# A planner that counts a shared port, with new durations, and integer additions that may run on VectorE

## The chip, the core and the metric

The kernel runs on one core of one Trainium2 chip. The core has five engines, each with its own queue of instructions that it takes in order: TensorE (PE in the rows, with its weight loads as PEld), VectorE (DVE), ScalarE (ACT), GpSimdE (POOL) and SyncE (SP, whose queue issues the DMAs). The metric is the device time of one execution in microseconds (us), the median of several runs.

## What is computed

Inputs are float32 for attention and 8-byte floats for the weights. For each of 4 batches and 8 heads, attention over 576 positions of width 64 keeps only scores within tau of the row's maximum; the 2304 tokens of width 512 that result go through two dense blocks:

```
scores = scale * np.matmul(q, k.transpose(0, 1, 3, 2))
thresh = np.max(scores, axis=-1, keepdims=True) - tau
scores = np.where(scores >= thresh, scores, -1e9)
x = softmax(scores) @ v                      # (2304, 512)
h = x @ w_in                                 # (2304, 2048)
x = (np.maximum(h, 0) + alpha * np.minimum(h, 0)) @ w_out
a, b = x @ w1, x @ w2                        # (2304, 1024) each
out = ((a * b) @ w3) @ w_out2                # (2304, 512)
```

## The kernel before

**Stages.** Attention comes first; its order of instructions is fixed by a table of numbers. The dense part follows on the same core, and the change is about that part. TensorE's first dense matmul starts 317 us after the first instruction.

**Tokens.** They are cut into five tiles: four of 512 (one for a batch) and one of 256 (the last 64 positions of each batch). The first dense stage takes them in the order 0, small tile, 1, 2, 3; the second in the order 0 to 3, small tile.

**Matmuls.** Each float32 operand is split into a high and a low part (hi and lo), and three products of parts stand for one product: 12 matmuls for a group of 128 rows of weights, 512 tokens and four blocks of 128. For each of 16 blocks f of the hidden width the first stage does a group "h" (x times w_in), then side (L925, ACT) and the leaky step (L930, DVE), both of which read PSUM, then hi and lo of the result g (helpers split_hi, L175 to L181, and split_lo, L184), and a group "acc" (times w_out). The second stage folds w3 and w_out2 into one matrix first, then does for 8 blocks a group for a, one for b, their product (L1047, L1050), its split, and a group of the output. The four or five rows named h, acc, gs, x, wa, wu and wp in the trace are these: h and acc are PSUM banks, x, gs the split activations, wa, wu, wp the split weights.

**Weights.** They arrive as 8-byte floats and are converted to float32 by integer operations: cvt_low (L192, ACT) brings the lower word to its place, cvt_high makes four steps on the upper word (L198 on ACT or L200 on DVE, then L203, L205, L209 on DVE), and cvt_round adds the two as integers (L214, on POOL always). The loads go into two buffers named raw, the result is a tile m of which there are three. Fourteen of the 16 blocks of w_in are converted during attention; the last two and the 16 of w_out while the first tile runs; w1, w2, w_out2 and w3, 40 tiles in all, behind that: these are converted once, stored to DRAM (L801) and loaded again later (z, L815). The 16 tiles of w3 are turned by TensorE before they are stored (four 128x128 transposes of a tile, L787).

**What sets the order.** A planner inside the kernel, list_order, makes the order of the dense part when the program is built. Each piece of work is an Op with the engines that can do it and a duration for each, a priority, the Ops it depends on, and the buffer it takes. The planner takes, again and again, the Op that can start first by its own clock (a little dearer where it has a choice of engines), puts it on the engine that starts it first, and so decides both the engine and the place in each engine's queue. On the chip every engine then follows its queue in that order and waits for what each instruction needs. The durations stand in the calls of op(...) in weight, halves, put_by, split and in the loops; MM is the time of one matmul of 512 columns. In the planner before, every engine is free when its own last Op has ended.

## Time and profile before

| what | value |
|---|---|
| median of 3 runs | 1092.97 us (1091.52 to 1093.36) |
| profiled execution, its own time | 1092.37 us |
| its span, first to last instruction | 1090.6 us |
| PE busy | 1047.3 us, 96% |
| DVE busy | 698.4 us, 64% |
| ACT busy | 440.0 us, 40% |
| POOL busy | 389.6 us, 36% |
| mean granted TensorE clock | 0.99 of full speed |

The shares are averages over stages with different limits: in attention all engines are busy, in the second dense stage hardly any but TensorE. What a stage loses is read from TensorE's rows in order of time: the start of one group of matmuls to the start of a later one, against the number of groups between. A matmul's own row overlaps the next one's by a little, so starts are compared, not durations. "Granted clock" is the share of full speed that the chip gave TensorE.

### The profile page before, as it was taken

What the parts mean: (1) busy time and instruction counts of PE and PEld (TensorE: products, weight loads), DVE (VectorE), ACT (ScalarE), POOL (GpSimd) and SP (SyncE); (2) the same over time, 40 slices, a digit from 0 to 9 for tenths busy, and PEclk for the clock granted to TensorE, in tenths of its full rate; (3) what the DMA queues carried; (4) which work ended last, traced back from release to release, by engine and by line L of the source; (5) the groups of instructions that cost most, each with busy time, mean ns of one, the idle gap of its engine ahead of it and who ended that gap; (6) DMA issues with size and microseconds to landing.
All of it is one profiled execution on the core that took longest, in us unless ns stands there. A gap on an engine that the chain in (4) does not pass through costs nothing.

```text
span 1090.6 us, 16110 instructions
## 1 busy us (share of the span) xinstructions
PE 1047.3 (96%) x5792; PEld 857.1 (79%) x5792; DVE 698.4 (64%) x1479; ACT 440.0 (40%) x840; POOL 389.6 (36%) x445
## 2 busy tenths in 40 slices
PE   4999999999989989999999999999999999999997
PEld 4877777777768769888867788888888888888896
DVE  5999999999869999987677545754322322223122
ACT  3989889898854443333233212211100201111020
POOL 3777787777543444544343112301200101000000
PEclk9999999999999998999989999999999999999999
DMA  3535252524213335545334202323100100001010
GB/s 93 148 85 145 78 153 77 149 81 130 51 59 109 104 116 170 178 156 181 107 137 145 78 1 58 97 68 97 39 1 1 39 1 10 29 1 39 1 39 20
DMA packets 62383, 89.14 MB, mean 82 GB/s; under 512 B 13920, under 2 KB 42592, under 8 KB 62304
## 3 DMA queue, kind: packets, MB, share of 16 engines
q1 hardware_dynamic: 60096, 88.10, 26.7%
q8 instruction: 46, 0.75, 0.3%
q10 hardware_dynamic: 2208, 0.01, 0.1%
q14 instruction: 33, 0.27, 0.1%
HBM read 62.40 MB, written 15.20 MB: 71 GB/s over the span
## 4 chain that ended last, share of the span: by engine, by line
PE 52%; DVE 4%; DMA 2%; POOL 1%; issue 1%; ACT 1%; SPq 0%; POOLq 0%; DVEq 0%; ACTq 0%
PE h L858 32%; PE acc L858 19%; DMA raw<-in_moe_w_dram 2%; POOL m L214 1%; DVE m L209 1%; DVE g L930 1%; DVE m L203 1%; DVE m L205 1%; DVE x L184 0%; PE h L787 0%; ACT raw L192 0%; DVE m L200 0%; ACT g L925 0%; DVE gs L181 0%; DVE gs L184 0%
## 5 line engine op out<-in xcount | busy, mean ns | idle before, releaser
L858 PE MATMUL h<-x,wa 128*128 128x512 f32 (+1 forms) x1920 | 418.4, 371 | 2.7 <-DVE x L184 1.3
L858 PEld LDWEIGHTS h<-x,wa 128*128 128x128 f32 x1920 | 337.4, 190 | 65.6 <-POOL x L184 2.2
L858 PE MATMUL acc<-gs,wu 128*128 128x512 f32 (+1 forms) x960 | 215.9, 373 | 9.4 <-POOL gs L184 4.8
L858 PEld LDWEIGHTS acc<-gs,wu 128*128 128x128 f32 x960 | 169.0, 190 | 44.8 <-POOL gs L184 8.3
L1050 DVE TENSOR_TENSOR ab<-h,ab 128x512 f32<-128x512 f32 (+1 forms) x40 | 25.5, 638 | 206.2 <-PE h L858 200.1
L184 POOL TENSOR_TENSOR x<-xT,x 128x512 fp32r<-128x512 f32 (+1 forms) x18 | 21.6, 1205 | 299.0 <-ACT x L179 251.7
L214 POOL TENSOR_TENSOR m<-m,raw 128x512 int32<-128x512 int32 x58 | 79.4, 1368 | 119.1 <-DVE m L209 86.8
L401 ACT ACTIVATE e<-s_ps,sm 128x576 f32<-128x576 f32 x144 | 107.1, 752 | 30.8 <-DVE sm L390 30.1
L438 POOL TENSOR_SCALAR p<-p,sm 128x576 f32<-128x576 f32 x128 | 94.1, 748 | 70.1 <-DVE sm L431 61.2
L390 DVE TENSOR_REDUCE sm<-s_ps 128x1 f32<-128x576 f32 x144 | 106.3, 747 | 19.2 <-PE s_ps L368 19.1
L1047 ACT COPY ab<-h 128x512 f32<-128x512 f32 (+1 forms) x38 | 20.6, 542 | 223.0 <-PE h L858 219.0
L858 PE MATMUL acc<-wp,gs 128*128 128x512 f32 x432 | 104.8, 390 | 0.9 <-DVE gs L181 0.9
L415 DVE SCALAR_TENSOR_TENSOR p<-s_ps,sm,e 128x576 f32<-128x576 f32 x128 | 101.9, 806 | 0.9 <-ACT e L401 0.6
L925 ACT ACTIVATE g<-h,sign_sb 128x512 f32<-128x512 f32 (+1 forms) x80 | 51.3, 641 | 120.4 <-PE h L858 102.2
L455 PE MATMUL pt_ps<-ident,p 128*128 128x128 f32 x576 | 89.6, 280 | 8.4 <-ACT pt L469 7.2
L858 PEld LDWEIGHTS acc<-wp,gs 128*128 128x128 f32 x432 | 80.5, 188 | 17.4 <-DVE gs L181 1.1
L482 PE MATMUL pv_ps<-pt,vraw 128*64 128x256 f32 (+1 forms) x640 | 84.5, 411 | 0.0
L368 PE MATMUL s_ps<-kT,qT 128*128 128x288 f32 x320 | 80.2, 333 | 3.5 <-DVE sm L393 1.7
L455 PEld LDWEIGHTS pt_ps<-ident,p 128*128 128x128 f32 x576 | 64.9, 141 | 21.0 <-ACT pt L469 11.8
L930 DVE SCALAR_TENSOR_TENSOR g<-h,salpha_sb,g 128x512 f32<-128x512 f32 (+1 forms) x80 | 55.5, 693 | 37.3 <-ACT g L925 37.2
L192 ACT ACTIVATE raw<-raw 128x512 int32<-128x512 uint32 x58 | 39.2, 679 | 81.8 <-DMA raw<-in_moe_w_dram 37.5
L368 PE MATMUL s_ps<-kT,qU 128*128 128x288 f32 x320 | 69.7, 300 | 2.3 <-DMA qU<-qT 2.3
(101 smaller groups left out, 1267.4 us busy)
## 6 DMA issues: line engine op xcount, KB each, us to landing
raw<-in_moe_w_dram SPq DMA_DIRECT2D x32, 512.0 KB, 3.8
raw<-in_moe_w_out_dram SPq DMA_DIRECT2D x24, 512.0 KB, 3.5
qU<-qT SPq DMA_DIRECT2D x32, 320.0 KB, 3.9
z<-w SPq DMA_DIRECT2D x40, 256.0 KB, 2.7
wraw<-in_moe_w_in_dram SPq DMA_DIRECT2D x14, 512.0 KB, 4.1
w<-m SPq DMA_DIRECT2D x24, 256.0 KB, 2.2
qraw<-in_q_dram SPq DMA_DIRECT2D x16, 256.0 KB, 4.1
kraw<-in_k_dram SPq DMA_DIRECT2D x16, 256.0 KB, 4.4
```

Of the source, the lines that this page charges most:

```text
L192: nc.scalar.activation(out=c, in_=low, func=AF.Copy, scale=2.0**-29)
L214: nc.gpsimd.tensor_tensor(out=mc[0], in0=mc[0], in1=mc[1], op=ALU.add)
L368: nc.tensor.matmul(out=sp[:, j, 0:HS], lhsT=d[t][:, hh, c * 128 : (c + 1) * 128], rhs=d["kT"][:, hh, k0 + j * HS : k0 + (j + 1) * HS], sta ...
L390: nc.vector.tensor_reduce(out=sm_of(u, 0), in_=st[u], axis=AX.XY, op=ALU.max, negate=True)
L401: nc.scalar.activation(out=es[u].rearrange("p (j s) -> p j s", j=2), in_=st[u], func=AF.Exp, bias=sm_of(u, 0))
L415: nc.vector.scalar_tensor_tensor(out=p_at(u).rearrange("p (j s) -> p j s", j=2), in0=st.pop(u), scalar=sm_of(u, 1), in1=es.pop(u).rearrang ...
L438: nc.gpsimd.tensor_scalar(out=out, in0=in_, scalar1=sm_of(u, 3), scalar2=1.0, op0=ALU.mult, op1=ALU.mult)
L455: nc.tensor.transpose(t[:, i, :], p[:, at + i * 128 : at + (i + 1) * 128], ident)
L482: nc.tensor.matmul(out=o[64 * hh : 64 * hh + 64, 0:n], lhsT=vr[:, hh, i, :], rhs=pt[:, 0 if i == 4 and not half else hh, i, :], start=(i = ...
L858: nc.tensor.matmul(out=out, lhsT=l, rhs=r, start=first and i == 0, stop=last and i == n - 1)
L925: nc.scalar.activation(out=gt()[:, 0:n], in_=ps()[:, 0:n], func=AF.Copy, scale=sign_sb[:, f : f + 1])
L930: nc.vector.scalar_tensor_tensor(out=gt()[:, 0:n], in0=ps()[:, 0:n], scalar=salpha_sb[:, f : f + 1], in1=gt()[:, 0:n], op0=ALU.mult, op1=A ...
```

## The change

Four things change in the planner and the calls, and nothing in what is computed.

1. Each Op has a mark, port, which is set for work that reads and writes SBUF alone and cleared where PSUM is read (copies from PSUM, the leaky step, the product of a and b, the split of the folded matrix). A marked Op on VectorE starts, by the planner's clock, only when the last marked Op on GpSimdE has ended, and the other way round.
2. The durations: a matmul 0.227 instead of 0.2163, work of 128x512 on GpSimdE 1.27 instead of 1.22, and on VectorE and ScalarE up to 0.07 more than before.
3. cvt_round takes an engine. In the dense part the planner may put the integer addition on GpSimdE (1.27) or VectorE (0.61). During attention it stays on GpSimdE.
4. Line numbers move by 6 above the planner's use (L184 becomes L190, L209 L215, L214 L220) and by 12 below (L858 becomes L870, L930 L942).

```diff
@@ list_order
+    shared = {"V": 0.0, "P": 0.0}
...
                 start = max([at, free_at.get(e, 0.0)] + ...)
+                if o.port and e in shared:
+                    start = max(start, shared["P" if e == "V" else "V"])
...
         free_at[e] = o.end
+        if o.port and e in shared:
+            shared[e] = o.end
@@ cvt_round
-    def cvt_round(mc):
-        nc.gpsimd.tensor_tensor(out=mc[0], in0=mc[0], in1=mc[1], op=ALU.add)
+    def cvt_round(eng, mc):
+        eng.tensor_tensor(out=mc[0], in0=mc[0], in1=mc[1], op=ALU.add)
         return mc[0].bitcast(F32)
@@ the dense part
-        MM = 0.2163
+        MM = 0.227
-        def op(engines, emit, prio, deps=(), take=None, free=()):
+        def op(engines, emit, prio, deps=(), take=None, free=(), port=True):
@@ weight
-            c = op({"A": 0.52}, low, prio, [ld])
+            c = op({"A": 0.57}, low, prio, [ld])
-            m = first = op({"V": 0.34, "A": 0.52}, lambda e: high(e, 0), prio, [ld], take="m")
+            m = first = op({"V": 0.34, "A": 0.55}, lambda e: high(e, 0), prio, [ld], take="m")
-                m = op({"V": 0.6 if i == 3 else 0.31}, ...)
-            a = op({"P": 1.22}, add, prio + 1, [c, m], free=[ld])
+                m = op({"V": 0.61 if i == 3 else 0.343}, ...)
+            a = op({"P": 1.27, "V": 0.61}, add, prio + 1, [c, m], free=[ld])
@@ halves
-            h = op({"A": 0.6} if signed else {"A": 0.52, "V": 0.335}, hi, ...)
-            l = op({"V": 0.6} if signed else {"P": 1.22, "V": 0.6}, lo, ...)
+            h = op({"A": 0.63} if signed else {"A": 0.52, "V": 0.336}, hi, ...)
+            l = op({"V": 0.665} if signed else {"P": 1.27, "V": 0.61}, lo, ...)
@@ split
-            lo_on = {"V": part(n, 0.66 if psum else 0.6)}
+            lo_on = {"V": part(n, 0.66 if psum else 0.61)}
             if not psum:
-                lo_on["P"] = part(n, 1.22)
+                lo_on["P"] = part(n, 1.27)
@@ first dense stage
-                u = op({"A": part(n, 0.57)}, side, now + 2.8, [hj], take="u")
-                g = op({"V": part(n, 0.61)}, prelu, now + 3.5, [u], free=[hj])
+                u = op({"A": part(n, 0.585)}, side, now + 2.8, [hj], take="u")
+                g = op({"V": part(n, 0.66)}, prelu, now + 3.5, [u], free=[hj], port=False)
```

How the order moves, at two places. In the names, m is a conversion's tile, raw its load, wu and wa split weights, gs and x split activations, g the leaky step's result, h a PSUM bank.

The first place is in the first token tile, where TensorE works on the blocks f while w_out is converted for later ones. VectorE's queue before, from one block to the next (two conversions, one split of gs):

```order
L203 TENSOR_SCALAR m_4869<-m_4869 128x512
L205 TENSOR_SCALAR m_4869<-m_4869 128x512
L209 SCALAR_TENSOR_TENSOR m_4869<-raw_4828,m_4869 128x512
L181 CAST gs_4890<-g_4865 128x512
L184 TENSOR_TENSOR gs_4890<-g_4865,gs_4890 128x512
L203 TENSOR_SCALAR m_4888<-m_4888 128x512
L205 TENSOR_SCALAR m_4888<-m_4888 128x512
L209 SCALAR_TENSOR_TENSOR m_4888<-raw_4850,m_4888 128x512
L758 SCALAR_TENSOR_TENSOR wu_4896<-m_4869,sign_sb_61,wu_4896 128x512
L930 SCALAR_TENSOR_TENSOR g_4913<-h_4873,salpha_sb_62,g_4913 128x512
```

GpSimdE's queue before, in the same stretch, with the additions of both conversions (m_4869, m_4888) and a subtraction of gs:

```order
L214 TENSOR_TENSOR m_4869<-m_4869,raw_4828 128x512
L214 TENSOR_TENSOR m_4888<-m_4888,raw_4850 128x512
L184 TENSOR_TENSOR gs_4935<-g_4913,gs_4935 128x512
L214 TENSOR_TENSOR m_4940<-m_4940,raw_4910 128x512
L214 TENSOR_TENSOR m_4962<-m_4962,raw_4920 128x512
```

VectorE's queue in the change, for the same two blocks of w_out (there m_4869 and m_4890):

```order
L215 SCALAR_TENSOR_TENSOR m_4869<-raw_4840,m_4869 128x512
L206 TENSOR_SCALAR m_4890<-raw_4862 128x512
L209 TENSOR_SCALAR m_4890<-m_4890 128x512
L211 TENSOR_SCALAR m_4890<-m_4890 128x512
L215 SCALAR_TENSOR_TENSOR m_4890<-raw_4862,m_4890 128x512
L942 SCALAR_TENSOR_TENSOR g_4906<-h_4871,salpha_sb_62,g_4906 128x512
L220 ISA m_4869<-raw_4840,m_4869 128x1024
L220 ISA m_4890<-raw_4862,m_4890 128x1024
L187 CAST gs_4930<-g_4906 128x512
L764 SCALAR_TENSOR_TENSOR wu_4926<-m_4869,sign_sb_61,wu_4926 128x512
L764 SCALAR_TENSOR_TENSOR wu_4932<-m_4890,sign_sb_61,wu_4932 128x512
L190 TENSOR_TENSOR gs_4930<-g_4906,gs_4930 128x512
```

GpSimdE's queue in the change, where the dense part begins:

```order
L220 TENSOR_TENSOR m_4647<-m_4647,raw_4617 128x512
L220 TENSOR_TENSOR m_4799<-m_4799,raw_4770 128x512
L190 TENSOR_TENSOR gs_4885<-g_4860,gs_4885 128x512
L220 TENSOR_TENSOR m_5026<-m_5026,raw_5000 128x512
L220 TENSOR_TENSOR m_5095<-m_5095,raw_5067 128x512
```

The additions of this pair have moved from GpSimdE to VectorE (the two ISA rows, which write the 512 words of m as 1024 half-words), and GpSimdE's queue, which held every conversion's addition in turn, goes from m_4647 to m_4799 and then to m_5026.

The second place is where tile 2 of the first dense stage begins. x is split anew, while w3 is converted and TensorE stands ready for a transpose. VectorE's queue before:

```order
L209 SCALAR_TENSOR_TENSOR m_6696<-raw_6649,m_6696 128x512
L181 CAST x_6734<-xT2_73 128x512
L181 CAST x_6736<-xT2_73 128x512
L930 SCALAR_TENSOR_TENSOR g_6732<-h_6706,salpha_sb_62,g_6732 128x512
L181 CAST x_6746<-xT2_73 128x512
L181 CAST gs_6750<-g_6732 128x512
L184 TENSOR_TENSOR x_6742<-xT2_73,x_6742 128x512
L203 TENSOR_SCALAR m_6748<-m_6748 128x512
L205 TENSOR_SCALAR m_6748<-m_6748 128x512
L209 SCALAR_TENSOR_TENSOR m_6748<-raw_6694,m_6748 128x512
L184 TENSOR_TENSOR gs_6750<-g_6732,gs_6750 128x512
```

GpSimdE's queue before, there:

```order
L214 TENSOR_TENSOR m_6696<-m_6696,raw_6649 128x512
L184 TENSOR_TENSOR x_6734<-xT2_73,x_6734 128x512
L184 TENSOR_TENSOR x_6736<-xT2_73,x_6736 128x512
L184 TENSOR_TENSOR x_6746<-xT2_73,x_6746 128x512
L214 TENSOR_TENSOR m_6748<-m_6748,raw_6694 128x512
L184 TENSOR_TENSOR gs_6804<-g_6781,gs_6804 128x512
```

VectorE's queue in the change (x_6731 to x_6739 are the same four parts of x):

```order
L215 SCALAR_TENSOR_TENSOR m_6722<-raw_6665,m_6722 128x512
L187 CAST x_6733<-xT2_73 128x512
L942 SCALAR_TENSOR_TENSOR g_6728<-h_6703,salpha_sb_62,g_6728 128x512
L220 ISA m_6722<-raw_6665,m_6722 128x1024
L190 TENSOR_TENSOR x_6731<-xT2_73,x_6731 128x512
L190 TENSOR_TENSOR x_6733<-xT2_73,x_6733 128x512
L190 TENSOR_TENSOR x_6737<-xT2_73,x_6737 128x512
L190 TENSOR_TENSOR x_6739<-xT2_73,x_6739 128x512
L190 TENSOR_TENSOR gs_6741<-g_6728,gs_6741 128x512
```

Three of the four subtractions of x have moved from GpSimdE to VectorE, behind the tile's last leaky step and the addition of the conversion that the next transpose reads; GpSimdE has no instruction at this place. In TensorE's queue of the change a group acc and a transpose stand between the last group h of the tile and the first of the next, and the acc that reads the last gs follows that.

## Rows read from the trace of the kernel before

**Rows 1.** Busy time by stage: engines' us (instructions), granted clock, DMA share, GB/s.
```profile
core 0: us, PE busy (x) PEld busy (x) DVE busy (x) ACT busy (x) POOL busy (x), PEclk, DMA share, GB/s
317.00:414.00 97.00, 90.13 (x376) 71.25 (x375) 90.86 (x128) 43.20 (x71) 42.67 (x31) 0.97 0.33 105
414.00:465.00 51.00, 48.39 (x384) 47.10 (x384) 46.95 (x86) 19.76 (x40) 22.86 (x19) 1.00 0.54 173
...
555.00:612.00 57.00, 52.46 (x230) 40.79 (x229) 41.12 (x63) 19.32 (x32) 21.98 (x17) 0.94 0.37 128
612.00:1086.00 474.00, 472.54 (x2174) 394.57 (x2172) 170.58 (x284) 67.63 (x114) 42.37 (x30) 1.00 0.10 32
```

**Rows 2.** TensorE in order of time, first and last dense matmuls: start, us, what.
```profile
317.12 0.97 PE L858 MATMUL h<-x,wa 128*128 128x512 f32 x3
...
1083.81 1.65 PE L858 MATMUL acc<-wp,gs 128*128 128x512 f32 x6 [0.92 <-DVE gs L181]
```

**Rows 3.** Chain that ended last, in order of time: start, us, what.
```profile
574.76 0.44 PE h L787 x4
...
620.39 2.72 PE h L858 x12
...
1067.30 1.43 PE h L858 x12
```

**Rows 4.** TensorE in order of time, end of the first tile.
```profile
362.45 2.88 PE L858 MATMUL h<-x,wa 128*128 128x512 f32 x12
...
407.33 0.56 PE L858 MATMUL acc<-gs,wu 128*128 128x512 f32 x1 [2.42 <-ACT gs L179]
408.87 5.06 PE L858 MATMUL acc<-gs,wu 128*128 128x512 f32 x11 [0.97 <-POOL gs L184]
413.73 0.63 PE L858 MATMUL h<-x,wa 128*128 128x256 f32 x2
```

**Rows 5.** TensorE in order of time, end of the small tile.
```profile
454.23 1.60 PE L858 MATMUL h<-x,wa 128*128 128x256 f32 x12
...
465.07 1.09 PE L858 MATMUL h<-x,wa 128*128 128x512 f32 x4
```

**Rows 6.** TensorE in order of time, w3's transposes (L787) among the groups.
```profile
553.72 1.39 PE L858 MATMUL h<-x,wa 128*128 128x512 f32 x4
...
557.71 2.43 PE L858 MATMUL h<-x,wa 128*128 128x512 f32 x5 [1.34 <-DVE x L184]
560.98 1.12 PE L787 MATMUL h<-ident,m 128*128 128x128 f32 x4 [0.84 <-POOL m L214]
...
611.95 5.72 PE L858 MATMUL h<-x,wa 128*128 128x512 f32 x24
```

**Rows 7.** All engines in order of time, 370 to 373.5 us.
```profile
370.54 1.42 POOL L214 TENSOR_TENSOR m<-m,raw 128x512 int32<-128x512 int32 x1 [0.63 <-DVE m L209]
370.83 1.42 DVE L203 TENSOR_SCALAR m<-m 128x512 f32<-128x512 f32 x1
...
372.28 0.43 DVE L205 TENSOR_SCALAR m<-m 128x512 int32<-128x512 int32 x1
372.74 0.69 DVE L209 SCALAR_TENSOR_TENSOR m<-raw,m 128x512 int32<-128x512 int32 x1
```

**Rows 8.** All engines in order of time, 353.9 to 356.5 us.
```profile
354.00 0.74 DVE L758 SCALAR_TENSOR_TENSOR wu<-m,sign_sb,wu 128x512 fp32r<-128x512 f32 x1
...
354.31 1.60 POOL L214 TENSOR_TENSOR m<-m,raw 128x512 int32<-128x512 int32 x1 [2.31 <-DVE m L209]
354.66 0.74 DVE L930 SCALAR_TENSOR_TENSOR g<-h,salpha_sb,g 128x512 f32<-128x512 f32 x1
```

**Rows 9.** VectorE by line and form, 620 to 1091 us: count, busy us, mean ns, idle before.
```profile
L184 DVE TENSOR_TENSOR gs<-g,gs 128x512 fp32r<-128x512 f32 x22 | 15.2, 690 | 0.5
...
L181 DVE CAST gs<-g 128x512 fp32r<-128x512 f32 x23 | 9.8, 426 | 22.6 <-PE acc L858 22.5
```

**Rows 10.** GpSimdE by line and form, 335 to 1091 us.
```profile
L214 POOL TENSOR_TENSOR m<-m,raw 128x512 int32<-128x512 int32 x55 | 75.1, 1366 | 112.4 <-DVE m L209 86.8 <-issue 8.3 <-ACT raw L192 7.6
```

**Rows 11.** GpSimdE in order of time, the step to tile 2.
```profile
552.69 2.66 POOL L184 TENSOR_TENSOR x<-xT,x 128x512 fp32r<-128x512 f32 x2 [0.36 <-DVE x L181]
...
559.32 1.61 POOL L214 TENSOR_TENSOR m<-m,raw 128x512 int32<-128x512 int32 x1 [2.21 <-DVE m L209]
```

More of the change, by code (lines that the diff above doesn't have):

```diff
@@ L25, with __init__ @@
 class Op:
-    def __init__(self, engines, emit, prio, deps=(), take=None, free=()):
-        self.engines, self.emit, self.prio, self.take = engines, emit, prio, take
+    def __init__(self, engines, emit, prio, deps=(), take=None, free=(), port=False):
+        self.engines, self.emit, self.prio, self.take, self.port = engines, emit, prio, take, port
         self.deps, self.free = list(dict.fromkeys(deps)), list(free)
@@ L703 @@
         NT = len(tiles)
-        MM = 0.2163
+        MM = 0.227
         ops = []
-        def op(engines, emit, prio, deps=(), take=None, free=()):
-            ops.append(Op(engines, emit, prio, deps, take, free))
+        def op(engines, emit, prio, deps=(), take=None, free=(), port=True):
+            ops.append(Op(engines, emit, prio, deps, take, free, port))
             return ops[-1]
@@ L794, in put_by @@
                 t = op({"T": 0.44}, tr, prio + 2, [a], take="h", free=[first])
-                a = first = op({"A": 0.48, "V": 0.6}, ev, prio + 3, [t], take="m", free=[t])
+                a = first = op({"A": 0.48, "V": 0.6}, ev, prio + 3, [t], take="m", free=[t], port=False)
             else:
@@ L974 @@
                 x_ready[t].append(
-                    op({"A": part(n, 0.48), "V": part(n, 0.6)}, ev, now + 1.5 * dt, [xj], free=[acc_op])
+                    op(
+                        {"A": part(n, 0.48), "V": part(n, 0.6)},
+                        ev,
+                        now + 1.5 * dt,
+                        [xj],
+                        free=[acc_op],
+                        port=False,
+                    )
                 )
@@ L1091, in store @@
                             nc.sync.dma_start(out=out[r0 : r0 + ST, :], in_=o()[64 * j : 64 * j + 64])
-                v = op({"A": 0.48, "V": 0.6}, ev, now + dt / 2 + 0.1 * m, [oj], take="u", free=[acc_op])
+                v = op({"A": 0.48, "V": 0.6}, ev, now + dt / 2 + 0.1 * m, [oj], take="u", free=[acc_op], port=False)
                 st_ = op({"S": 0.65 if t < B else 1.3}, store, now + dt / 2 + 0.5, [v])
```

22 lines of the change are left out of this document (14 added, 8 removed).

## The prediction, made before the changed kernel was run

> **What bounds the kernel now.** I read the busy table by stage first, then TensorE's row of instructions in order of time, then VectorE and GpSimdE beside each other. The reader is to see that TensorE sets the end: in the dense part it works from 317.12 us to 1083.81 + 1.65 = 1085.46 us [rows 2], 768.3 us. The work there is fixed. The first stage has 16 blocks x 4 tiles x 24 matmuls of 512 columns and 16 x 24 of 256; the second has 192 and 4 x 8 x 36 of 512, and 8 x 24 of 256 with 8 x 6 of 512 for the small tile; together 2928 of 512 columns, 576 of 256, and 16 transposes of a 512-column block. Twelve of 512 columns take 2.72 us, twelve of 256 1.43 to 1.44 (I take 1.44), a block's transposes 0.44 [rows 3]: 244 x 2.72 + 48 x 1.44 + 16 x 0.44 = 739.8 us. So 28.5 us of the dense part are lost, and they lie in few places:
>
> - End of the first token tile: from 362.45 to 413.73 [rows 4] there are 15 groups of twelve, 40.8 us in 51.3: **10.5 us lost**. The waits named are for ACT gs and POOL gs, the split of the activations, and eleven matmuls then take 5.06 us instead of 2.5: the granted clock is down (0.97 over the stage [rows 1], at half speed for a while after the long wait).
> - Small tile to next tile: 454.23 to 465.07 [rows 5], 5 groups of 1.44 in 10.84 us: **3.6 us lost**.
> - Conversions of w3, with TensorE's transposes among the matmuls: 553.72 to 611.95 [rows 6], 16 groups and 10 transposes, 43.5 + 4.4 in 58.2 us: **10.3 us lost**, with a wait for DVE x, one for POOL m (the conversion's addition), and half clock again (0.94 in this stage [rows 1]).
>
> That makes 24.4 us; the other 4.1 us lie at the first matmuls, the last group and in small pieces, and from 612 us on TensorE is busy 472.5 of 474 us [rows 1].
>
> Why the partners are late is in the two engines' rows. A POOL addition starts at 370.54 and takes 1.42; the DVE instruction that starts at 370.83 takes 1.42 and ends when POOL does, where the same kind takes 0.43 just after [rows 7]. A DVE instruction that reads PSUM (L930) takes 0.74 in the middle of a POOL addition [rows 8]: it is not held. So SBUF-to-SBUF work of the two engines goes one after the other, and POOL's price is 1.37 for an addition [rows 10] where DVE has 0.69 for a subtraction of the same size [rows 9].
>
> **The change, part by part.** Attention's order is untouched; only the dense part's order moves. The order shows 44 of its 58 integer additions on DVE, and 48 fewer subtractions on POOL (of 128x512 and 128x256). I set demand against supply, in each place as (DVE time) + (POOL time) with nothing beside nothing, and again without the L930 rows, which POOL can run beside.
>
> *First tile, from its first to its 16th L930:* supply is 15 steps x 5.44 = 81.6 us. Prices: L200, L203, L205 0.43, L209 0.69 [rows 7], L758 0.74, L930 0.74 [rows 8], the cast (hi) 0.43, the subtraction (lo) 0.69 [rows 9], POOL 1.37 [rows 10].
> Before: 50 x 0.43 + 18 x 0.69 + 16 x 0.74 + 15 x 0.74 + 10 hi x 0.43 + 9 lo x 0.69 = 67.3 on DVE, 26 x 1.37 = 35.6 on POOL: 91.8 without L930, 102.9 with it, over the supply by 10.2 to 21.3. The 10.5 us lost sit at the lower end, which says that L930 really hides.
> After: 47 x 0.43 + 16 x 0.69 + 15 x 0.74 + 15 x 0.74 + 7 x 0.43 + 16 lo x 0.69 + 13 additions = 67.5 + 13 x 0.69 = 76.5 on DVE, 5 x 1.37 = 6.9 on POOL: 72.3 without L930, 83.4 with it: between 9.3 us to spare and 1.8 too much. At the end where before sits, nothing is lost; I leave 1.0 us for bunches (the order puts eight conversion instructions between two L930). **Gain 9.5.**
>
> *The addition's own price* is the one unknown: no row has an integer addition on DVE, and the order shows it as an instruction of another form that writes 1024 half-words. It reads and writes the same bytes as L209 (every second word of raw, and m, 512 results), 0.69; as twice as many elements it would be 2 x 0.69 = 1.38. I take 0.69, since L209 is the nearest row, and keep 1.38 as a rival. The strided operand costs nothing by the rows: L209 at 0.69 is no slower than the contiguous subtraction at 0.69. The Trainium skill (Vector Engine (DVE) Microarchitecture Reference, section 5.2, Measured stream behaviour on trn2) says otherwise: a port keeps its full rate only on pairs of adjacent words, and one source that hops at every element gives 1.73 ns a column, an estimate of 512 x 1.73 + 75 ns = 0.96 us; by it the first tile's additions would cost 3.5 us more, inside what is to spare, and w3's transposes some 2 us, about 1076 in all. The trace disagrees with it on L209, and the trace decides.
>
> *Small tile to next tile:* the change runs three of the four subtractions of x and most of gs on DVE, and TensorE has five groups of 1.44 to cover them instead of four. Three lo and one hi on DVE are 2.5 us and one lo on POOL 1.37, together 3.9 under 7.2 us, beside gs of the small tile. I leave 1.5 of 3.6 us. **Gain 2.1.**
>
> *w3's stretch:* at the step to the third large tile POOL did three subtractions of x, two of them for 2.66 us from 552.69 [rows 11], and the addition that the transpose waits for came behind them. In the changed order the addition and all four lo follow on DVE: behind the tile's last h come ACT 0.7, L930 0.74, addition 0.69, four lo 2.8, gs lo 0.69 = 5.6 us, and TensorE has a group, a transpose and a group to do meanwhile, 2.72 + 0.44 + 2.72 = 5.9. It fits by 0.3 us, so small waits stay; ten or more transposes stand singly between groups and each can wait a little. No wait comes near the 2.4 and 1.3 us [rows 4, 6] behind which the clock fell. I leave 3.0 of 10.3 us. **Gain 7.3.**
>
> *At nothing:* the eight subtractions of wu moved to DVE lie after 612 us, where DVE is busy 171 of 474 us [rows 1]; if that cover failed it would cost 8 x 0.69 = 5.5 us. The new durations and the new time of a matmul in the planner act through the order alone. Casts moved to ACT (ten of gs in the first tile instead of nine, two of wa) cost ACT little; it is busy 43 of 97 us there [rows 1].
>
> Sum: 9.5 + 2.1 + 7.3 = 18.9. The profiled execution took 1092.37 us, 0.6 below the median of the runs, 1092.97; 1092.4 - 18.9 = **1073.5 us**. If all 24.4 went, and with them a little of the rest, 1067.
>
> **Rivals.**
>
> 1. *The addition costs 1.38.* For it: 1024 elements written; against: the bytes are L209's. The first tile's demand rises by 13 x 0.69 = 9.0 us, from 9.3 to spare to 0.3 at the lower end; I put 3 us of loss. Each transpose of w3 waits directly for an addition: 16 x 0.69 = 11 us at most, half of it 5.5, with 3 us as in the forecast and a half-clock stretch of 3.4 (0.06 of 57 us [rows 1]). With 2.5 at the small tile, 17 of 24.4 us stay: about 1085. The Trainium skill (VectorE: DVE Perf Modes, Mode 2x_1P) gives 16-bit operands with step 1 two results a cycle, which would make 1024 half-words as quick as 512 words and the sum the forecast's; no row here shows that mode.
>
> 2. *The clock falls once more at w3.* The fit of 0.3 us fails: a raw load lands late, or the two raw buffers hold a conversion up, and one wait of over 2 us brings a half-clock stretch. For it: in this stretch the changed order gives TensorE's transposes no slack. Price 3 + 3.4: about 1080.
>
> 3. *Slower: VectorE becomes the bound.* The mechanism is the same addition at a far higher price, in place of POOL's 1.37. Room is 9.3 us in the first tile (13 additions) and, by the same sum without L930, 3 in the small tile (5 additions, 46 us of supply for 43) and 12 in the second large one (17 additions, 91 for 79 us). The 24.4 us are eaten when 35 (p - 0.69) = 24.4 + 24.3, at p = 2.1 us; at 2.5 it would be 35 x 1.81 - 48.7 = 14.7 us slower, about 1107. For it: a form no row shows. Against: nothing of 512 words on DVE takes over 0.75 unheld.
>
> 4. *No change:* the lost time is the conversions' loads, not the port. Against: the waits name POOL and DVE results, and the held instructions end with POOL's. About 1092.
>
> **How the numbers follow.** Forecast (1067 to 1078) 0.62; clock falls 0.14; addition at 1.38 0.12; no change 0.05; slower 0.07. The first three are faster: 0.88. A measurement of this kernel tells about 0.2%, 2.2 us, from no change: same 0.05, slower 0.07. The range runs from 1067, all waits gone, to 1086, which takes in the 1.38 case; the last two cases and the worst of rival 1 are left out, less than 2 in 10.
>
> **What would show it.** Right: the DVE addition near 0.69; L203 back at 0.43 on the mean; POOL busy far less before 612 us, DVE about as much as before; no half clock around 410 us; the stretch of the first tile at 5.44 us a step; TensorE's dense part some 749 us long. Wrong: an addition over 1.2 us, TensorE waiting for DVE gs in the first tile (DVE the bound), or 10 us still lost among the transposes (the loads, or the planned places of the transposes, set that stretch, not the port).

## The result, and the profile after

The changed kernel takes 1105.24 us (median of 4 runs, 1104.30 to 1106.07) against 1092.84 for the kernel before (4 runs): a ratio of 1.011, 95% interval 1.0098 to 1.0122. It is **slower by 12.4 us**, where 1073.5 and "faster" had been forecast, and lies outside the range of 1067 to 1086. (Of the kernel of run 6 below, one execution of six took 2271.55 us, twice the others, and is left out.)

To see where the time went I took, in both traces, each dense matmul's start to the next one's start, less what it takes in full swing (2.72 / 12 us for 512 columns, 1.436 / 12 for 256, 0.44 / 4 for a transpose), and summed that by place:

| us that TensorE lost | before | forecast | after |
|---|---|---|---|
| start of the dense part | 1.7 | 1.7 | 1.8 |
| first tile, and the small one up to 440 us | 10.9 | 1.4 | 2.6 |
| small tile's end | 3.8 | 1.7 | 6.5 |
| w3's transposes | 10.5 | 3.2 | 13.2 |
| second dense stage, its tiles' ends | 0.2 | 0.2 | **16.3** |
| last groups | 1.4 | 1.4 | 0.4 |
| all of the dense part | 28.5 | 9.6 | 40.8 |

(The forecast column is before less the gains that the prediction gave.) The difference of the sums, 12.3 us, is that of the times. So one term came out nearly as forecast, two had the wrong sign, and the largest stood in the prediction "at nothing". Of the 31.2 us between the forecast loss and the measured one 16.1 are in the second dense stage, 10.0 among w3's transposes and 4.8 at the small tile's end.

Busy time by stage of the changed kernel, columns as in [rows 1]; the third row takes two of the stages there together, and the last ends later since the kernel does:

```profile
core 0: us, PE busy (x) PEld busy (x) DVE busy (x) ACT busy (x) POOL busy (x), PEclk, DMA share, GB/s
317.00:414.00 97.00, 95.82 (x446) 78.66 (x443) 89.23 (x163) 47.90 (x80) 11.89 (x10) 1.00 0.35 114
414.00:465.00 51.00, 46.70 (x346) 45.18 (x346) 37.32 (x78) 17.55 (x37) 5.38 (x4) 0.93 0.44 135
465.00:612.00 147.00, 137.55 (x624) 110.33 (x623) 114.43 (x206) 53.31 (x86) 9.62 (x7) 1.00 0.48 158
612.00:1100.00 488.00, 477.09 (x2163) 396.09 (x2161) 169.34 (x301) 65.07 (x110) 16.43 (x13) 0.99 0.09 29
```

In the first row POOL has fallen from 42.7 us [rows 1] to 11.9, TensorE is busy 95.8 of 97 at full clock, and VectorE is busy about as long as before (89.2 us, 90.9 before). VectorE by line and form (count, busy us, mean ns, idle before), 317 to 1100 us, answers to [rows 9]:

```profile
L215 DVE SCALAR_TENSOR_TENSOR m<-raw,m 128x512 int32<-128x512 int32 x58 | 41.8, 724 | 1.3
...
L220 DVE CUSTOM_DVE_ANT_0 m<-raw,m 128x1024 uint16<-128x1024 uint16 x44 | 31.1, 712 | 1.3
...
L209 DVE TENSOR_SCALAR m<-m 128x512 f32<-128x512 f32 x58 | 27.2, 472 | 5.2 <-ACT m L204 2.5 <-issue 1.5
```

The addition (L220) costs 712 ns in the mean, so the one unknown price was taken rightly. TensorE in order of time, at the first and the second step from one token tile to the next in the second stage:

```profile
850.86 2.57 PE L870 MATMUL acc<-wp,gs 128*128 128x512 f32 x10 [1.11 <-DVE gs L190]
...
910.38 2.88 PE L870 MATMUL acc<-wp,gs 128*128 128x512 f32 x12
913.10 2.88 PE L870 MATMUL h<-x,wa 128*128 128x512 f32 x12
917.50 0.73 PE L870 MATMUL acc<-wp,gs 128*128 128x512 f32 x2 [1.52 <-DVE gs L187]
919.91 4.64 PE L870 MATMUL acc<-wp,gs 128*128 128x512 f32 x10 [1.67 <-DVE gs L190]
924.35 5.87 PE L870 MATMUL h<-x,wa 128*128 128x512 f32 x22
```

At 917.50 and 919.91 TensorE waits twice for the split of the tile's last product, and the ten matmuls behind that take 4.4 us where ten take 2.27: the granted clock is at its half level, 1.2 of 2.4 GHz. The busy time by stretch (columns as above) says the same, for this step and for the next, 72 us later:

```profile
919.00:925.80 6.80, 5.89 (x14) 4.65 (x15) 2.15 (x4) 0.00 (x0) 0.00 (x0) 0.50 0.11 41
990.60:997.40 6.80, 5.68 (x13) 4.47 (x14) 2.35 (x4) 0.00 (x0) 0.00 (x0) 0.50 0.10 39
```

VectorE in order of time, at the same step, shows why that split is late: x of the next tile goes first.

```profile
916.09 0.69 DVE L1069 TENSOR_TENSOR ab<-h,ab 128x512 f32<-128x512 f32 x1 [6.28 <-PE h L870]
916.70 0.42 DVE L187 CAST x<-xT 128x512 fp32r<-128x512 f32 x1
917.03 0.42 DVE L187 CAST gs<-ab 128x512 fp32r<-128x512 f32 x1
917.37 1.89 DVE L190 TENSOR_TENSOR x<-xT,x 128x512 fp32r<-128x512 f32 x3
919.17 0.68 DVE L190 TENSOR_TENSOR gs<-ab,gs 128x512 fp32r<-128x512 f32 x1
```

In the kernel before nothing waits there:

```profile
914.02 2.88 PE L858 MATMUL acc<-wp,gs 128*128 128x512 f32 x12
916.74 2.88 PE L858 MATMUL h<-x,wa 128*128 128x512 f32 x12
919.46 2.88 PE L858 MATMUL acc<-wp,gs 128*128 128x512 f32 x12
```

The work on VectorE is nearly the same; TensorE's order is not. With a and b for the two groups h of a block, [f] for the output group of block f, and a dash for the next tile, TensorE's rows have at the four steps from tile to tile (the fourth leads to the small tile):

```
before, steps 1 and 4      a7 b7 [6] a0' b0' [7]
before, steps 2 and 3      a7 b7 [6] a0' [7] b0'
changed, step 1            a7 b7 [6] [7] a0' b0'
changed, steps 2 and 3     a7 [6] b7 [7] a0' b0'
changed, step 4            a7 [6] b7 a0' b0' [7]
```

x of the next tile can be split only when b7 has ended, since it takes the buffers of the old x. Before, [6] covers that, and a0' covers the split of the last product. In the changed order nothing stands between b7 and [7], which reads that split, at steps 2 and 3, and nothing between b7 and a0' at step 4. The four steps lose 1.4, 6.5, 6.5 and 1.9 us.

### The profile page after: what moved, and what is told of

Same layout as the page of the kernel before. It is cut to its first block, busy times and chain, and to the rows that moved or that the text cites. A ratio compares the mean times of both kernels' runs of the same rounds, so it can differ in the third digit from the quotient of the medians.

```text
span 1103.4 us, 16003 instructions
## 1 busy us (share of the span) xinstructions
PE 1051.9 (95%) x5792; PEld 859.8 (78%) x5792; DVE 690.8 (63%) x1560; ACT 447.0 (41%) x851; POOL 263.2 (24%) x353
## 4 chain that ended last, share of the span: by engine, by line
PE 72%; DVE 12%; DMA 7%; ACT 6%; issue 2%; POOL 0%; SPq 0%; ACTq 0%; DVEq 0%; POOLq 0%
PE h L870 31%; PE acc L870 19%; PE pv_ps L488 7%; PE s_ps L374 7%; PE pt_ps L461 5%; DMA raw<-in_moe_w_dram 4%; ACT pt L475 3%; PE tr L302 2%; DVE m L215 2%; DMA raw<-in_moe_w_out_dram 2%; ACT kT L324 1%; DVE m L211 1%; DVE gs L190 1%; DVE m L209 1%; DVE m L220 1%
## 5 line engine op out<-in xcount | busy, mean ns | idle before, releaser
L870 PE MATMUL h<-x,wa 128*128 128x512 f32 (+1 forms) x1920 | 415.7, 370 | 2.0 <-DVE x L190 1.8
L870 PEld LDWEIGHTS h<-x,wa 128*128 128x128 f32 x1920 | 336.8, 189 | 64.2 <-DVE x L190 2.6
L870 PE MATMUL acc<-gs,wu 128*128 128x512 f32 (+1 forms) x960 | 215.8, 374 | 13.2 <-DVE gs L190 10.3
L870 PEld LDWEIGHTS acc<-gs,wu 128*128 128x128 f32 x960 | 169.6, 192 | 48.2 <-DVE gs L190 13.7
L870 PE MATMUL acc<-wp,gs 128*128 128x512 f32 x432 | 109.6, 402 | 7.5 <-DVE gs L190 4.5
L870 PEld LDWEIGHTS acc<-wp,gs 128*128 128x128 f32 x432 | 82.9, 194 | 26.5 <-DVE gs L190 5.7
L461 PE MATMUL pt_ps<-ident,p 128*128 128x128 f32 x576 | 89.2, 278 | 8.4 <-ACT pt L475 7.2
L461 PEld LDWEIGHTS pt_ps<-ident,p 128*128 128x128 f32 x576 | 64.5, 140 | 21.2 <-ACT pt L475 11.9
L942 DVE SCALAR_TENSOR_TENSOR g<-h,salpha_sb,g 128x512 f32<-128x512 f32 (+1 forms) x80 | 55.5, 694 | 39.7 <-ACT g L937 39.5
L475 ACT COPY pt<-pt_ps 128x512 f32<-128x512 f32 x128 | 70.4, 591 | 3.8 <-PE pt_ps L461 2.0
L190 POOL TENSOR_TENSOR gs<-ab,gs 128x256 fp32r<-128x256 f32 x1 | 0.7, 737 | 286.3 <-DVE gs L187 286.3
L488 PEld LDWEIGHTS pv_ps<-pt,vraw 128*64 128x64 f32 x640 | 43.2, 137 | 30.5 <-issue 2.6
```

The lines of the kernel that those rows point to most:

```text
L461: nc.tensor.transpose(t[:, i, :], p[:, at + i * 128 : at + (i + 1) * 128], ident)
L475: nc.scalar.copy(out=pt[:, g, 0:4, to], in_=ps)
L488: nc.tensor.matmul(out=o[64 * hh : 64 * hh + 64, 0:n], lhsT=vr[:, hh, i, :], rhs=pt[:, 0 if i == 4 and not half else hh, i, :], start=(i = ...
L870: nc.tensor.matmul(out=out, lhsT=l, rhs=r, start=first and i == 0, stop=last and i == n - 1)
L942: nc.vector.scalar_tensor_tensor(out=gt()[:, 0:n], in0=ps()[:, 0:n], scalar=salpha_sb[:, f : f + 1], in1=gt()[:, 0:n], op0=ALU.mult, op1=A ...
```

## The experiments

The theory to test, **A**: the planner, which by its new clock sees the four subtractions of x one after the other, puts [7] ahead of a0'; and with the longer matmul it puts [6] ahead of b7; TensorE then waits and falls to half clock. Rivals: **B**, VectorE's load is too high in itself; **C**, the rule of the port alone is to blame. Further letters stand in the expectations. Ratios are to the kernel before, with 95% intervals.

**1. A matmul at 0.2163 in the second stage alone** (label mm2)

```diff
         w12_k, w12_ops, wo2_k, wo2_ops = {}, {}, [], []
+        MM = 0.2163
```

> The changed kernel with a matmul at 0.2163 instead of 0.227 in the planner for the second dense stage alone. The order up to the end of the first stage stays the changed kernel's; in the second stage the last output group but one, [6], comes behind the tile's last group b again, and the last one, [7], behind it, ahead of the next tile's first group a. Theory A (what is lost in the second stage is decided by how many groups stand between a tile's last b and the next tile's first a; where only [7] is left, TensorE waits for its split and falls to half clock): each of the three boundaries costs about 1.4 us, as the first one does in the changed kernel, 4.2 in place of 16.3: 1093. Theory B (VectorE has too much work in the second stage): the load is the same, so 1105. Theory C (the rule of the port alone is to blame, with any duration): the rule still stands, 1105.

Measured: 1093.22 us, ratio 0.9995 (0.9981 to 1.001). The second stage loses 3.6 us in place of 16.3, as A said (4.2, 1093). B and C, which said 1105, fall. TensorE at the second step:

```profile
907.18 5.60 PE L870 MATMUL h<-x,wa 128*128 128x512 f32 x24
912.62 3.33 PE L870 MATMUL acc<-wp,gs 128*128 128x512 f32 x14
916.71 2.58 PE L870 MATMUL acc<-wp,gs 128*128 128x512 f32 x10 [0.76 <-DVE gs L190]
```

a7 b7 stand together, [6] and [7] behind them; one short wait is left, and the clock stays up (1.00 from 910 to 925 us).

**2. No port mark in the second stage** (label s2noport)

```diff
-            xs, xl = split_x(t, now - 3, x_ready[t])
+            xs, xl = split_x(t, now - 3, x_ready[t], shared=False)
-... now + 2 * dt / 3 + 0.7, [g], "gs", free=[ca])
+... now + 2 * dt / 3 + 0.7, [g], "gs", free=[ca], shared=False)
```

(shared=False clears port in the two Ops of split.)

> The changed kernel with the port mark cleared for the splits of x and gs in the second dense stage alone; durations as changed. The order there: the next tile's first group a stands between the last b and the last output group, but [6] still comes ahead of the last b at the second and third boundary. Theory A: those two boundaries have nothing between the last b and the next a, which needs four splits that start only when b has ended: about 4 us of wait each and a half-clock stretch of 3.4 each, with the first boundary clean: 14 to 16 us lost, 1102 to 1106. Theory C (the rule of the port is what costs): the loss goes, 1089. Theory B (VectorE's load): a subtraction more on GpSimdE, a little better, 1100 or more.

Measured: 1097.60, ratio 1.0047 (1.0032 to 1.0062). The first step is clean, as A said, and the others still cost, so C is wrong; but A's price was too high:

```profile
909.59 3.97 PE L870 MATMUL h<-x,wa 128*128 128x512 f32 x16
914.59 0.96 PE L870 MATMUL h<-x,wa 128*128 128x512 f32 x3 [1.04 <-DVE x L190]
916.28 1.43 PE L870 MATMUL h<-x,wa 128*128 128x512 f32 x5 [0.72 <-DVE x L190]
```

The order here is a7 [6] b7 a0' [7] b0'. The group a0' starts with the first part of x and goes on, a few matmuls at a time, as the parts come: 2.5 us are lost, not 4, and no half clock follows. The step to the small tile costs 3.5, with one wait of 1.78 us and a granted clock of 0.57 behind it (1050 to 1054 us); 8.7 in all.

**3. Both in the second stage** (label mm2s2): the two diffs above together.

> Both edits together: in the second dense stage alone no port mark for the splits of x and gs, and a matmul at 0.2163. The first boundary between token tiles is then ordered as in the kernel before; at the second and third, [6] comes ahead of the next a, which stands ahead of [7]: b7 [6] a0 [7]. Theory A: nothing or under 1 us is lost at each boundary, 1089 to 1091, below the kernel before by what the first token tile gained and the first stage's other places lost. Theory B: 1100 or more. Theory C: 1089.

Measured: 1089.32, ratio 0.9957 (0.9945 to 0.997). 0.3 us are lost in the second stage. The order at all four steps is that of the kernel before, and the loss that stands in the table's fifth line is gone. So A holds: what was lost is the place of two groups, put there by two parts of the change together. Which part moves which is read from the orders of runs 1 and 2: with the mark alone [7] stands ahead of a0', with the longer matmul alone [6] ahead of b7. Undoing the matmul's time there gives back 12.0 us, undoing the mark 7.6, undoing both 15.9.

**4. Additions on VectorE alone** (label p0d0v1): the changed kernel without the rule, and with all durations and MM as before.

```diff
-    shared = {"V": 0.0, "P": 0.0}
+    shared = {}
-        MM = 0.227
+        MM = 0.2163
...
-            a = op({"P": 1.27, "V": 0.61}, add, prio + 1, [c, m], free=[ld])
+            a = op({"P": 1.22, "V": 0.6}, add, prio + 1, [c, m], free=[ld])
```

> The kernel before with one part of the change: integer additions of the dense part may run on VectorE (the planner puts 32 there); no port in the planner, the old durations. The second stage's boundaries are ordered b7 [6] a0 [7] or with b0 between, as before. Theory A: nothing lost there; in the first tile the planner still takes the two engines for independent, so part of the 10.5 us stays: 1085 to 1093. Theory C: the same. Theory B (additions on VectorE make it the bound): slower than the kernel before, 1095 or more.

Measured: 1092.81, ratio 0.9991 (0.998 to 1.0002): no gain. The planner put 32 additions on VectorE, but L209 (L203 before, 701 ns there before 612 us) still takes 648 ns in the mean, where an unheld one takes 0.43 us, and by 430 us the dense part has lost 15.0 us, where the kernel before had lost 12.6. Permission alone, without the rule and the new durations, is worth nothing here.

**5. Additions on GpSimdE alone** (label addpool): the changed kernel with

```diff
-            a = op({"P": 1.27, "V": 0.61}, add, prio + 1, [c, m], free=[ld])
+            a = op({"P": 1.27}, add, prio + 1, [c, m], free=[ld])
```

> The changed kernel with every integer addition on GpSimdE again; port rule and durations stay. Theory L (the first tile's gain needs the additions on VectorE): by the prediction's sum 67.5 us of VectorE without additions and 18 x 1.37 of GpSimdE, 81.1 without L942 against a supply of 81.6, with no room for bunches: half or more of the 9.6 us gained there is lost again, and w3's conversions wait for GpSimdE, so 1110 to 1120. Theory M (it is the rule of the port that gives the gain, by keeping subtractions off GpSimdE): the first tile stays within 2 us of the changed kernel, 1103 to 1107.

Measured: 1130.79, ratio 1.0342 (1.0325 to 1.0359). The first tile's gain is lost, as L said, but not by L's cause; M falls, and the time is worse than both. The losses are 22.4 us in the first tile, 12.0 around the small tile's end and 15.9 in w3's stretch. TensorE in the first tile:

```profile
362.93 0.39 PE L870 MATMUL acc<-gs,wu 128*128 128x512 f32 x1
382.79 4.32 PE L870 MATMUL acc<-gs,wu 128*128 128x512 f32 x11 [19.47 <-DVE gs L190]
```

One wait of 19.5 us: on VectorE the subtraction of gs (382.05) stands behind the steps of seven conversions (the first at 355.83), and those come every 4 us, since each needs a raw buffer that GpSimdE's addition gives back. Neither engine is full in that time: GpSimdE idles 2.7 of every 4 us, VectorE about 1. So it is a place in a queue, which the planner's clock did not see as late (that last part is inferred). The rule needs the freedom to use VectorE as much as the freedom needs the rule.

**6. The mark only in the first tile** (label np1, and once more for its trace as np1_again): on mm2s2 (weight has a shared of its own, which sets port of its Ops):

```diff
-            box, a, first = weight(src, prio)
+            box, a, first = weight(src, prio, shared=False)
-            xs, xl = split_x(t, now - 3, [])
+            xs, xl = split_x(t, now - 3, [], shared=t == 0)
-                h, l = split(..., gs, now + 4.3, [g], "gs", free=[u])
+                h, l = split(..., gs, now + 4.3, [g], "gs", free=[u], shared=t == 0)
```

> The kernel with both second-stage edits (label mm2s2), and the port mark left only where the first token tile is worked on: cleared for x and gs of the other tiles and for the conversions of w1, w2, w_out2 and w3. The first tile's order stays. Theory F (in the small tile and among the transposes of w3 it is the port's rule, which puts nearly all work on VectorE, that loses more than before): the places cost what they cost in the kernel before, 3.6 and 10.3 us in place of 5.5 and 13: about 1084. Theory H (the conversions of w3 come too densely for VectorE, on whichever engine their additions are): the first of the two gets better, the second does not: 1087 to 1090.

> The kernel of the run np1 once more, for its profile: np1 took 1116.8 us where mm2s2 took 1089.3. Theory F2 (without the rule, conversions outside the first tile send additions and subtractions to GpSimdE beside VectorE's work, and at 4 us a conversion both engines' work goes one after the other): the loss of TensorE lies in w3's stretch, 30 us or more in place of 13, with instructions of VectorE held for 1.3 us or longer. Theory K (an accident of the order, such as one late load or the clock): the loss lies in one or two places, with half clock.

Measured: 1115.45 (median of three; 1116.82 with the one left out), ratio 1.0207 (1.0186 to 1.0228), and 1115.03 (2 runs), 1.0197 (1.0177 to 1.0218). F falls: it was to be 1084; H's 1087 to 1090 is missed too. Without the rule the dense part loses 49.7 us: 32 in w3's stretch (500 to 630 us), as F2 expected, but also 5.6 in one place at the small tile's beginning (415 us), with half clock in both (0.95 from 500 to 630 us, 0.59 from 417 to 424.5). With conversions 4 us apart the rule earns its keep in the first stage.

**7. w3's conversions 6 us apart** (label sp6), on mm2s2:

```diff
-            put_by(key, src, 24 * MM * NF + 5 + 4 * i, key[0] == "3")
+            put_by(key, src, 24 * MM * NF + 5 + 4 * i + 2 * max(0, i - 23), key[0] == "3")
```

> mm2s2 with the planned time between two conversions of w3 6 us instead of 4 (their 16 priorities spread). Theory H: at 4 us a conversion needs 3 x 0.43 + 2 x 0.69 = 2.7 us of VectorE, so a block of 5.44 us of TensorE's work with 1.36 transposes of 0.44 asks for 3.6 + 0.74 + 1.12 = 5.5 us of VectorE in 6.0, before copies of y and the splits of x: no room; at 6 us 2.4 + 1.9 = 4.3 in 5.8. The 13 us of the stretch fall to 4 or less, 1080. Theory F: the rule still stands, 1087 to 1090. Theory G (each wait there comes from the steps of a conversion standing ahead of gs's subtraction in VectorE's queue, which the planner does since the subtraction has two engines and is ranked 0.21 us later): fewer conversions, so fewer waits of the same length, about two thirds: 1085.

Measured: **1075.70**, ratio 0.9837 (0.9822 to 0.9852). The loss among the transposes, 15.5 us in mm2s2, is 0.8. Busy time by stretch, mm2s2 first and then sp6:

```profile
465.00:612.00 147.00, 135.83 (x615) 108.61 (x614) 112.71 (x205) 52.34 (x84) 9.57 (x7) 1.00 0.47 155
```

```profile
465.00:612.00 147.00, 147.00 (x678) 121.46 (x677) 117.23 (x213) 52.12 (x82) 12.59 (x9) 1.00 0.46 150
```

VectorE does more work in the same time, and TensorE never waits. So the planned distance of the transposes' conversions, which the change did not touch, decides this stretch. That VectorE's mean load (H's sum) is the reason is not shown: it was busy 112.7 of 147 us when TensorE waited. A rival stands: the distance moves the loads of w3, VectorE's steps and the transposes all at once, and at 4 us the loads are on the path too. In mm2s2 a load of 512 KB lands 4.0 us after its issue (median), there are two raw buffers, and between 518 and 606 us these loads, five of them, make up 27% of the chain that ended last. Two of the five (start, us, what):

```profile
530.15 5.82 DMA raw<-in_moe_w_dram
564.62 5.53 DMA raw<-in_moe_w_dram
```

In sp6 that chain holds nothing but TensorE's work in the same stretch. Which of the three it is stays open.

**8. gs's subtraction ahead of the conversions' steps** (label gsb), on mm2s2:

```diff
                 h, l = split(..., gs, now + 4.3, [g], "gs", free=[u])
+                l.bias = -0.5
```

> mm2s2 with a bias of -0.5 us in the ranking of gs's subtraction in the first dense stage, so that it goes ahead of a conversion's steps. Theory G: of the eight waits of 1.0 to 1.4 us for this subtraction in w3's stretch two or three steps of 0.43 each go away: 6 to 8 us less, 1082. Theory H: what TensorE doesn't wait for at gs it waits for at the transposes: 1087 to 1090.

The grounds for G were these rows of the changed kernel, VectorE and TensorE in order of time: the subtraction that TensorE waits 1.20 us for stands behind three steps of a conversion. (The expectation counts eight such waits; the rows of mm2s2 have five of 1.0 us or more for this subtraction in w3's stretch.)

```profile
571.67 0.42 DVE L209 TENSOR_SCALAR m<-m 128x512 f32<-128x512 f32 x1
572.13 0.43 DVE L211 TENSOR_SCALAR m<-m 128x512 int32<-128x512 int32 x1
572.59 0.69 DVE L215 SCALAR_TENSOR_TENSOR m<-raw,m 128x512 int32<-128x512 int32 x1
573.20 0.68 DVE L190 TENSOR_TENSOR gs<-g,gs 128x512 fp32r<-128x512 f32 x1
```

```profile
573.94 2.79 PE L870 MATMUL acc<-gs,wu 128*128 128x512 f32 x11 [1.20 <-DVE gs L190]
```

Measured: 1093.78, ratio 1.0007 (0.9997 to 1.0016): 4.5 us worse than mm2s2; G's time and H's both miss. The stretch from 510 to 610 us loses 19.9 us, 7.0 of them between 560 and 570. What G named did happen: in w3's stretch the waits for this subtraction are down to one of 0.23 us. But two long waits have come, and both stand behind a load. TensorE, then VectorE and ScalarE in order of time:

```profile
523.93 0.72 PE L793 MATMUL h<-ident,m 128*128 128x128 f32 x4 [4.69 <-DVE m L220]
566.87 5.62 PE L870 MATMUL acc<-gs,wu 128*128 128x512 f32 x12 [4.58 <-ACT gs L185]
```

```profile
520.97 0.43 DVE L206 TENSOR_SCALAR m<-raw 128x512 int32<-128x512 int32 x1 [2.03 <-DMA raw<-in_moe_w_dram]
```

```profile
565.66 0.65 ACT L198 ACTIVATE raw<-raw 128x512 int32<-128x512 uint32 x1 [2.69 <-DMA raw<-in_moe_w_dram]
```

The transpose at 523.93 waits for the conversion that VectorE could begin only at 520.97. The cast of gs (566.22, ScalarE) stands in the queue behind a conversion's step that waited 2.69 us for its load.

**9. Both, with 8 us** (label sp8gsb): the bias, and

```diff
-            put_by(key, src, 24 * MM * NF + 5 + 4 * i, key[0] == "3")
+            put_by(key, src, 24 * MM * NF + 5 + 4 * i + 4 * max(0, i - 23), key[0] == "3")
```

> mm2s2 with both: 8 us between two conversions of w3, and the bias on gs's subtraction. Theories G and H: nearly all of w3's 13 us and some of the small tile's 5: 1073 to 1078. If neither holds (the places of the transposes themselves, or the loads, cost the time): 1085 or more.

Measured: 1076.62, ratio 0.9844 (0.9829 to 0.9859): not told apart from sp6. G and H had the same forecast here, so their hit does not choose between them.

**10. The small tile's end without the mark** (label sp6x), on sp6:

```diff
-            xs, xl = split_x(t, now - 3, [])
+            xs, xl = split_x(t, now - 3, [], shared=t == 0)
```

> sp6 with the port mark cleared for the splits of x in the first dense stage's tiles behind the first. The next tile's first group h then stands ahead of the small tile's last output group, as in the kernel before. If the loss of 5.1 us at the small tile's end in sp6 has the cause of the boundaries in the second stage (nothing but the last output groups left ahead of the next tile's h, a wait, half clock), it falls to the kernel before's 3.6 or to 1.7 without half clock: 1072 to 1074.5. If it is VectorE's load, nothing: 1075.7.

Measured: 1081.12, ratio 0.9883 (0.9867 to 0.99), slower than sp6 by 5 us; neither branch. By 440 us it has lost 8.3 us, sp6 4.5 (the mark is cleared at the small tile's beginning too), and at the small tile's end 6.4, sp6 5.2. GpSimdE and then VectorE in order of time, at the small tile's end, show what the rule keeps away:

```profile
452.49 5.92 POOL L190 TENSOR_TENSOR x<-xT,x 128x512 fp32r<-128x512 f32 x4 [10.64 <-ACT x L185]
```

```profile
452.69 1.51 DVE L187 CAST x<-xT 128x512 fp32r<-128x512 f32 x1
454.13 1.75 DVE L215 SCALAR_TENSOR_TENSOR m<-raw,m 128x512 int32<-128x512 int32 x1
455.80 1.48 DVE L190 TENSOR_TENSOR gs<-g,gs 128x256 fp32r<-128x256 f32 x1
457.20 1.76 DVE L220 CUSTOM_DVE_ANT_0 m<-raw,m 128x1024 uint16<-128x1024 uint16 x1
...
459.28 0.41 DVE L190 TENSOR_TENSOR gs<-g,gs 128x256 fp32r<-128x256 f32 x1
```

Four instructions of VectorE are held, each ending 0.3 to 0.6 us behind one of GpSimdE's four, the subtraction of gs among them with 1.48 us instead of 0.41; TensorE waits 3.14 us for it, and the granted clock is 0.58 from 457 to 464 us.

**11. x on VectorE alone** (label sp6v), on sp6:

```diff
-            if not psum:
+            if not psum and pool:
                 lo_on["P"] = part(n, 1.27)
-            xs, xl = split_x(t, now - 3, [])
+            xs, xl = split_x(t, now - 3, [], pool=t in (0, B))
```

> sp6 with GpSimdE taken out for the subtractions of x in the first dense stage's three large tiles behind the small one: all four on VectorE. In sp6x four of them on GpSimdE held four instructions of VectorE for 1.5 to 1.8 us each, gs's subtraction among them, and the small tile's end lost 6 us there; in sp6 one held one, and it lost 5.1. If the shared port and the half clock behind its waits are the cause, no instruction is held here; the order now has four groups h of the next tile between the small tile's last four output groups, and the loss falls to 2 us or less: 1071 to 1073. If VectorE's own load is the cause (four subtractions, 2.8 us, ahead of gs), TensorE waits as long as before: 1075 or more.

Measured: 1076.96, ratio 0.9864 (0.9847 to 0.9881). The order has the groups between each other, and the half clock is gone (1.00 from 440 to 470 us):

```profile
450.41 0.50 PE L870 MATMUL h<-x,wa 128*128 128x512 f32 x1 [0.34 <-ACT x L185]
...
455.32 1.58 PE L870 MATMUL acc<-gs,wu 128*128 128x256 f32 x11 [0.59 <-DVE gs L190]
456.73 2.91 PE L870 MATMUL h<-x,wa 128*128 128x512 f32 x12
```

From 440 to 470 us 3.8 are lost where sp6 loses 5.2, but 1.5 more at 518 us, where the order moved too; the dense part loses 12.4 in all, and 12.0 in sp6. The place got better, the kernel did not, and the 1071 to 1073 were a miss.

Of all versions **sp6 is the fastest by its median**, 1.6% below the kernel before and 2.7% below the changed one by the two ratios (0.9837 / 1.011). sp8gsb and sp6v are too near it to be told apart. It keeps the whole change in the first stage and adds the wider distance of w3's conversions.

## Why the prediction was wrong

**The first tile: right.** Forecast a gain of 9.5 us, measured 8.3 in the table's row. Of the 2.6 us left there, 1.6 are one wait in the small tile, at 429 us, for a subtraction of gs that took 1.50 us beside an addition on GpSimdE (428.96, 1.34); at the first tile's end 0.9 are left. The demand by the two engines' sums told this place well, the half clock at 407 us is gone, and L209 (L203 before) has come from 701 ns in the mean (317 to 612 us) to 472.

**The addition's price: right**, 0.712 us for the 0.69 taken from L209. Rivals 1 and 3 (1.38; 2.1 and more) fall. The Trainium skill's rule on single strided words (Vector Engine (DVE) Microarchitecture Reference, section 5.2), by the prediction's estimate 0.96 us, does not hold for this instruction in this trace; nor for L215, 0.724. The Trainium skill's 1.73 ns a column stands there for hops of 4 KiB; the step here is 8 bytes.

**Rival 3 was taken for the only way to be slower, and that is not what came.** VectorE has no more to do after the change: it is busy 690.8 us in all, 698.4 before.

**At nothing: the step that failed.** The prediction costed what lies behind 612 us by VectorE's load there, and gave 5.5 us if the cover failed; the second stage lost 16.3. It did not read TensorE's own order behind 612 us, although the change gives the planner a new matmul time and a new clock for the splits. The cover is not VectorE's idle time: it is the groups that stand between the instruction that makes work possible (b7's end, the last product) and the group that reads it. Two groups moved, and the 16.3 us came of it, some 5.8 of them through the clock by an estimate (half of the 5.9 and 5.7 us of work in the two stretches at half clock above). Runs 1 to 3 show it from three sides. That the new durations act through the order alone was true, and was the reason to look. This step is the largest but not the only one: with the second stage's order given back (run 3) the kernel takes 1089.32 us, still above the range.

**w3's stretch: wrong in sign**, gain 7.3 forecast, loss 2.7. The prediction took the loss there for the port's, saw that TensorE's transposes had 0.3 us to spare and left 3.0 us of waits. Rival 2 said that the fit would fail, by one long wait and one half clock; instead there is no half clock (1.00 in the third row of the busy times by stage) but seven waits of 0.9 to 1.4 us, five of them for gs's subtraction. Runs 3 and 7 show what decides the place under the rule: 15.5 us lost with conversions 4 us apart, 0.8 with 6. The prediction's own last sentence had that ("the loads, or the planned places of the transposes, set that stretch, not the port") as what would make it wrong. Whether it is the loads, the transposes' places or VectorE's queue stays open, and so does the port's share: at 4 us the place lost 10.5 us in the kernel before, 10 in run 4 and 32 in run 6, all without the rule there, and 6 us without the rule was not tried.

**The small tile's end: wrong in sign**, gain 2.1 forecast, loss 2.7. Three subtractions and a cast of x on VectorE were counted at 2.5 us, under five groups of TensorE. But those five are the small tile's last output groups, and they wait for gs themselves. TensorE, GpSimdE and VectorE in order of time:

```profile
451.79 0.38 PE L870 MATMUL acc<-gs,wu 128*128 128x256 f32 x1 [0.86 <-ACT gs L185]
453.70 2.10 PE L870 MATMUL acc<-gs,wu 128*128 128x256 f32 x12 [1.52 <-DVE gs L190]
456.30 5.27 PE L870 MATMUL acc<-gs,wu 128*128 128x256 f32 x23 [0.51 <-DVE gs L190]
```

```profile
450.99 1.43 POOL L190 TENSOR_TENSOR x<-xT,x 128x512 fp32r<-128x512 f32 x1 [10.02 <-ACT x L185]
```

```profile
451.20 1.50 DVE L187 CAST x<-xT 128x512 fp32r<-128x512 f32 x1
```

The cast of x, which stands in VectorE's queue ahead of gs's subtraction (453.23), is held by the one subtraction left on GpSimdE, and the clock falls to its half level at 454.7 us. It is the same kind of place as in the second stage: behind the small tile's last h only output groups are left. Run 10 shows that giving x back to GpSimdE makes it worse, run 11 that taking it off GpSimdE altogether brings 5.2 us to 3.8.

The terms that were right came from adding up prices per engine. The terms that were wrong were all at a seam between two tiles or two kinds of work. At the second stage's steps the runs show that not the sum but the order of a few instructions decides; at the other two that is argued.

## What to carry to other kernels

When a planner's costs change, compare the order on the bottleneck engine in every stage, the idle-looking ones too, and at each seam between tiles count what stands between the last reader of a buffer and the first group that needs its new contents. A rule that makes the model truer (instructions are held: run 10) can still make the order worse, since the old error may have put a covering group in the right place; so try each part alone and in each stage. With the second stage's order held the change gained 3.9 us, and with w3's conversions farther apart as well 17.5; what that spacing alone would give the kernel before was not tried.

## What the runs showed of the hardware

- An integer addition on VectorE of two 128x512 tiles, one with every second word, takes 0.69 us unheld (686 ns in the mean in sp6 from 465 to 640 us, 712 in the changed kernel's dense part); on GpSimdE 1.37 (the kernel before, [rows 10]).
- A held instruction of VectorE ends shortly behind GpSimdE's: in run 10, 0.3 to 0.6 us behind, a cast with one input, a subtraction, a conversion's step and the addition, 1.48 to 1.76 us each; the instruction that reads PSUM (L942) took 0.74 at 573.80 in the changed kernel, as ever, while GpSimdE added from 573.59 for 1.46. The Trainium skill (SBUF — State Buffer, section "SBUF: two separate sides") calls the shared pair an exclusive lock that is held for a whole instruction, against two inputs in SBUF or a mode with two ports. The trace agrees for two inputs in SBUF (the subtraction 1.48, the addition 1.76) and for one with PSUM (0.74, not held); that the cast runs in such a mode no run here shows.
- The clock fell to its half level, for 6.8 us, at 919.0 us in the changed kernel, in the second of two waits of 1.52 and 1.67 us with two matmuls between. It fell too within a wait of 3.14 us (run 10, 456 us) and just behind a single one of 1.78 (run 2, 1050 us). It did not behind single waits of 1.11 and 1.61 us (850 and 1060 us in the changed kernel), behind 1.04 and 0.72 (run 2), nor in the changed kernel's w3 stretch, with seven waits of 0.9 to 1.4 us in 80. What tells these apart was not tried.
